# Two due times in a planned attention-plus-MLP kernel: VectorE's normalisations of the last pairs, and GpSimd's scales of the later batches

## The chip, the core and the metric

The kernel runs on one core of one Trainium2 chip. The metric is the device time of one execution in microseconds (us), as the median of several executions. One execution in each set was also profiled; all lines below come from those profiles. The names in the lines: PE is TensorE, PEld its weight loads, DVE is VectorE, ACT is ScalarE, POOL is GpSimd, SP is SyncE, which issues most transfers.

## The reference, cut to what matters

```python
q, k, v: (8, 12, 448, 64) float32          # batch, heads, tokens, head size
q_n, k_n = q / |q|, k / |k|
attn = softmax(q_n @ k_n.T / 0.1)           # per batch and head
x    = concat_heads(attn @ v)               # (3584, 768)
h    = x @ w_in                             # (768, 2048)
out  = (h * sigmoid(1.702 * h)) @ w_out     # (2048, 768)
```

## The kernel before

Two heads make a *pair*; a batch has six pairs, so pairs 0 to 5 are batch 0, 6 to 11 batch 1, and so on. For each pair: load k and q, square (ScalarE), sum (VectorE), take the root, invert, scale k and q to unit length, transpose, make the scores (TensorE), exponentiate (ScalarE), multiply with v (TensorE), normalise (VectorE), turn (TensorE), copy. When all pairs of a batch are there, the MLP takes its tokens. Batch 0 and 1 are worked in two halves of the tokens ("h" is 0 or 1), and the first MLP matmul of batch 0 is made in eight *units* for each half.

Nothing in the program decides the order by hand. A planner in the kernel simulates the engines before the program is written: each operation has an engine, an assumed duration, a due time, things it must follow, and slots that it takes and frees (PSUM banks, buffers, and a "port" shared by VectorE and GpSimd). Whenever an engine is free in that simulation, it gets the *ready* operation with the earliest due time. The result is a fixed order of instructions for each engine. In the cut below, `s` and `sh` are a pair's own place in time, `early` lies before it, `first` means a pair of batch 0, `URGENT` is 12; due times are in units of the plan, not in us, and a smaller one goes first.

```python
plan = Plan(dict(q=NQK, k=NQK, v=4, sq=3, qks=6, vt=NV, qkT=7, sp=2, a=1, exp=NE, xs=3, xf=3)
          | dict(x=2 * HP, mm=3, run=3, th=3, g0=KT2, g1=KT2, ost=2, port=1))   # mm: 3 PSUM banks, ost: 2 output buffers
...
add(("scale", ti, x), "DVE" if dve else "POOL", 0.7 if dve else 1.0,
    early + 0.5 if first else s - 5 - ti * 0.1, partial(scale, x, ti, ...),
    after=[("norm", 1, grp)], takes=[("qks", 1), ("port", 1)], frees=[(nm, 1), ("port", 1)])
...
if x == grp[0] and x in range(HP, PW):                # pairs 6 to 9: the root on GpSimd
    add(("norm", 0, grp), "POOL", 0.5 + 2.4 * n, early + 0.3, partial(power, grp), after=reds)
    add(("norm", 1, grp), "DVE", 0.45, early + 0.3, partial(inverse, grp), after=[("norm", 0, grp)], **port)
...
add(("nx", x, h), "DVE", 0.65, sh + 1 - (0 if first else URGENT), partial(normalise_h, x, h), after=[("at", x, h)], ...)
add(("turn", x, h), "PE", 0.15, sh + 1, partial(turn_h, x, h), after=[("nx", x, h)], ...)
add(("x", x, h), ..., 0.35, sh + 1 - (0 if first else URGENT), partial(turned_h, x, h), after=[("turn", x, h)], ...)
...
add(("ost", b2, t, n), "ACT", 0.4, due - URGENT, partial(halve, b2, t, n), after=after,   # evacuates an output tile
    takes=[("ost", int(n == 0))], frees=[("mm", 1)], ...)
add(("w_out", i), "POOL", 1.0, 3 + i, partial(load_w_out, i), ...)                         # two halves of w_out
```

In the lines, L581 is the first MLP matmul of batch 0, L534 and L552 that of the later batches, L611 the second MLP matmul, L484 the product with v, L507 the turn, L375 a dummy transpose ("fill") that the kernel issues to keep TensorE warm, L495 and L497 the normalisation, L517 the copy after the turn, L591 and L568 the gate (it frees a PSUM bank), L563 the tanh, L269 the sums of squares, L326 the root on GpSimd, L333 and L334 its inverse, L343 the scale, L623 the evacuation of an output tile.

## Time and profile before

| | before |
|---|---|
| time | 432.85 us, median of 3 (432.06 to 433.2) |
| TensorE busy | 98% of a span of 430.0 us, granted clock 1.00 |
| VectorE, ScalarE, GpSimd busy | 55%, 68%, 41% |
| fills on TensorE | 238, of these 47 after 44 us |
| TensorE from 100 us to the last matmul | full but for some tenths of a us |

The lines themselves, and what they leave to win, are in the prediction.

### The profile page before, as it was taken

To read this page: it belongs to the slowest core of one execution; us is meant where nothing else is said; L and a number is where in the kernel's file an instruction comes from. 1 tells how busy PE (TensorE), PEld (TensorE's weight loads), DVE (VectorE), ACT (ScalarE), POOL (GpSimd) and SP (SyncE) were. 2 spreads that over 40 slices of the span, in tenths; PEclk is the share of its full clock that TensorE was granted. 3 is DMA by queue.
4 is the path that set the end of the run, shared out by engine and by line. 5 is a ranking of instruction groups with operands and counts; after the bars stand their busy time and mean duration, and the time that the engine had idled before them with its cause. 6 is when DMAs were issued, how large, how long until landed. Compare 5 with 4: busy or idle time off the path is not lost.

```text
span 430.0 us, 11091 instructions
## 1 busy us (share of the span) xinstructions
PE 419.9 (98%) x4438; PEld 261.2 (61%) x4438; DVE 236.5 (55%) x621; ACT 290.5 (68%) x460; POOL 175.4 (41%) x229
## 2 busy tenths in 40 slices
PE   7889999999999999999999999999999999999996
PEld 7768886654565555555556556556656556555564
DVE  5875887877874577829656554553432433123200
ACT  5979679958877788887884886766673864233321
POOL 0830995297678847463682717260100000000000
PEclk9999999999999999999999999999999999999999
DMA  8999997968999999696979475845203021211122
GB/s 215 197 202 268 246 204 207 291 128 203 207 201 184 249 236 204 160 196 169 162 197 220 123 201 134 152 107 93 63 14 93 9 63 49 50 38 37 38 73 75
DMA packets 98099, 64.03 MB, mean 149 GB/s; under 512 B 56320, under 2 KB 93056, under 8 KB 98048
## 3 DMA queue, kind: packets, MB, share of 16 engines
q1 hardware_dynamic: 92320, 57.03, 58.2%
q0 software_dynamic: 5696, 6.29, 8.9%
q8 instruction: 35, 0.57, 0.5%
q14 instruction: 16, 0.13, 0.1%
q10 hardware_dynamic: 32, 0.01, 0.0%
HBM read 45.61 MB, written 11.01 MB: 132 GB/s over the span
## 4 chain that ended last, share of the span: by engine, by line
PE 86%; ACT 4%; DVE 3%; issue 2%; POOL 2%; DMA 1%; SPq 0%; ACTq 0%; POOLq 0%
PE mm L611 34%; PE mm L534 17%; PE mm L552 11%; PE avp L431 8%; PE sp L405 7%; PE sp L467 2%; PE mm L484 2%; ACT et L416 2%; PE mm L581 2%; DMA k<-in_k_dram 1%; ACT sq L263 1%; DVE n L269 1%; POOL qks L343 1%; PE tps L375 1%; POOL n L326 1%
## 5 line engine op out<-in xcount | busy, mean ns | idle before, releaser
L416 ACT ACTIVATE et<-sp 112x896 f16<-112x896 f32 x192 | 170.1, 919 | 29.7 <-PE sp L405 24.8
L611 PE MATMUL mm<-w_out,gT 128*128 128x384 f16 (+1 forms) x912 | 158.4, 323 | 0.0
L611 PEld LDWEIGHTS <-gT 128*128 128x128 f16 x912 | 83.9, 98 | 60.6 <-issue 11.0
L568 DVE SCALAR_TENSOR_TENSOR gT<-th,mm 128x448 f16<-128x448 f16 x112 | 67.0, 616 | 64.9 <-ACT th L563 64.8
L563 ACT ACTIVATE th<-mm 128x448 f16<-128x448 f32 x128 | 67.7, 550 | 39.3 <-PE mm L534 31.9
L534 PE MATMUL mm<-xT,w_in 128*128 128x448 f16 x408 | 85.2, 353 | 0.3 <-DVE gT L568 0.3
L269 DVE TENSOR_REDUCE n<-sq 112x8 f32<-112x512 f32 x96 | 63.9, 679 | 21.8 <-ACT sq L263 13.2
L623 ACT ACTIVATE ost<-mm 128x384 f32<-128x384 f32 (+1 forms) x57 | 27.8, 488 | 62.1 <-PE mm L611 61.7
L534 PEld LDWEIGHTS <-w_in 128*128 128x128 f16 x408 | 37.7, 98 | 36.8 <-issue 5.8
L552 PE MATMUL mm<-xT,w_in 64*128 64x448 f16 x528 | 57.1, 349 | 0.0
L359 POOL CAST vt<-v 112x256 f16<-112x256 f32 x90 | 34.0, 404 | 56.4 <-PE avp L431 42.2
L431 PEld LDWEIGHTS <-et 112*128 112x128 f16 x1152 | 43.6, 97 | 13.8 <-issue 3.7
L343 POOL TENSOR_TENSOR qks<-k,y 112x512 f16<-112x512 f32 x38 | 39.7, 1044 | 26.3 <-DVE y L310 12.9
L431 PE MATMUL avp<-vt,et 112*128 112x65 f16 x1152 | 47.0, 193 | 0.1
L442 DVE RECIPROCAL rcx<-avp 128x4 f32<-128x4 f32 x72 | 13.0, 180 | 61.7 <-PE avp L431 61.6
L262 POOL TENSOR_TENSOR sq<-q 112x512 f32<-112x512 f32 x33 | 34.2, 1041 | 29.4 <-DVE y L310 9.0
L405 PE MATMUL sp<-qkT 64*128 64x448 f16 x288 | 43.3, 353 | 0.0
L343 POOL TENSOR_TENSOR qks<-q,y 112x512 f16<-112x512 f32 x38 | 39.7, 1044 | 0.0
L552 PEld LDWEIGHTS <-w_in 64*128 64x128 f16 x528 | 25.6, 94 | 21.0
L263 ACT ACTIVATE sq<-k 112x512 f32<-112x512 f32 x48 | 30.3, 635 | 3.4 <-DMA k<-in_k_dram 3.4
L445 DVE TENSOR_TENSOR xf<-avp,rcx 128x256 f16<-128x256 f32 x72 | 30.6, 425 | 2.5
L405 PEld LDWEIGHTS <-qkT 64*128 64x128 f16 x288 | 13.4, 93 | 14.6 <-issue 6.7
(48 smaller groups left out, 277.6 us busy)
## 6 DMA issues: line engine op xcount, KB each, us to landing
k<-in_k_dram SPq DMA_DIRECT2D x48, 224.0 KB, 4.5
q<-in_q_dram SPq DMA_DIRECT2D x48, 224.0 KB, 5.0
v<-in_v_dram SPq DMA_DIRECT2D x48, 224.0 KB, 4.2
w_in<-in_moe_w_in_dram POOLq DMA_DIRECT2D x2, 1536.0 KB, 15.7
w_out<-in_moe_w_out_dram POOLq DMA_DIRECT2D x2, 1536.0 KB, 15.4
out_dram<-ost SPq DMA_DIRECT2D x7, 336.0 KB, 4.7
out_dram<-ost SPq DMA_DIRECT2D x8, 288.0 KB, 2.9
out_dram<-ost SPq DMA_DIRECT2D x8, 240.0 KB, 3.1
```

The costliest lines, as they stand in the source:

```text
L262: return nc.gpsimd.tensor_tensor(out=sqs[x, ti], in0=src, in1=src, op=ALU.mult)
L263: return nc.scalar.activation(out=sqs[x, ti], in_=src, func=AF.Square)
L269: nc.vector.tensor_reduce(out=n2s[grp][:, x - grp[0], ti], in_=sqs.pop((x, ti)), axis=AX.X, op=ALU.add,)
L343: return eng.tensor_tensor(out=qkss[x][:, 1 - ti].rearrange("p c j d -> p j c d"), in0=src, in1=rss[x][:, ti, :, :, None].to_broadcast((P, ...
L405: nc.tensor.matmul(out=sp[:, j, :S], lhsT=keys(x, j, c), rhs=queries(x, j, 0, S), start=True, stop=True,)
L416: nc.scalar.activation(out=e[:, : 2 * S].rearrange("p (j s) -> p j s", j=2), in_=sps.pop(key)[:P, :, :S], func=AF.Exp, scale=inv_tau, **kw,)
L431: nc.tensor.matmul(out=ps[:, (D + 1) * t : (D + 1) * (t + 1)], lhsT=exps[x, c][:, q0 : q0 + 128], rhs=values(x, c, D * j, D * j + D + 1), ...
L534: nc.tensor.matmul(out=ps[:, :S], lhsT=w_in_sb[:, kk, 128 * m : 128 * (m + 1)], rhs=xTs[b, kk][:, :S], start=(kk == 0), stop=(kk == KT1 - 1),)
L552: insts.append(nc.tensor.matmul(out=mms[b, m + i][:, :S], lhsT=w_in_sb[rows, kk, 128 * (m + i) : 128 * (m + i + 1)], rhs=xTs[b, kk][rows, :S],
L563: nc.scalar.activation(out=ths[key], in_=mms[key][:, :S], func=AF.Tanh, scale=0.851)
L568: nc.vector.scalar_tensor_tensor(out=gT[:, m, (b % 2) * S : (b % 2 + 1) * S], in0=ths.pop((b, m)), scalar=1.0, in1=mms.pop((b, m))[:, :S], ...
L611: nc.tensor.matmul(out=mms[b2, t, n][:, : c1 - c0], lhsT=gT[:, kk, 128 * t : 128 * (t + 1)], rhs=w_out_sb[:, kk, c0:c1], start=(kk == 0), ...
```

## The change

Two intents: let the last two pairs of batch 0 go first on VectorE, as the second half of the MLP of batch 0 waits for them; and on GpSimd let the scales of a pair go ahead of the root of the next.

```diff
-    PW = 10
+    PW = (6, 7, 8, 9)
...
-    groups += [(x,) for x in range(HP, PW)] + [tuple(range(PW, HALF))] * (PW < HALF)
+    groups += [(6,), (7,), (8,), (9,), (10, 11)]
...
-   ... early + 0.5 if first else s - 5 - ti * 0.1,          # due time of the scales
+   ... early + 0.5 if first else s - 8 - ti * 0.1,
...
-        if x == grp[0] and x in range(HP, PW):
+        if x == grp[0] and x in PW:
...
-   add(("nx", x, h), ..., sh + 1 - (0 if first else URGENT), ...
+   add(("nx", x, h), ..., sh + 1 - (0 if first and not (h and x >= HP - 2) else URGENT), ...
...
-   add(("x", x, h), ..., sh + 1 - (0 if first else URGENT), ...
+   add(("x", x, h), ..., sh + 1 - (0 if first and not (h and x >= HP - 2) else URGENT), ...
```

## The prediction

> **What bounds the kernel now.** I began with the page of the kernel before: busy shares and the slices.
>
> ```profile
> span 430.0 us, 11091 instructions
> PE 419.9 (98%) x4438; PEld 261.2 (61%) x4438; DVE 236.5 (55%) x621; ACT 290.5 (68%) x460; POOL 175.4 (41%) x229
> PE   7889999999999999999999999999999999999996
> PEclk9999999999999999999999999999999999999999
> ```
>
> TensorE is busy 419.9 of 430.0 us at full clock, so only 10.1 us of the span are open to any reordering. Splitting the span into stretches shows where they lie: 3.5 us in the first 20 us (before the change can act), 2.2 us between 20 and 50, 0.5 between 50 and 100, about 0.2 between 100 and 300, and 3.6 in the tail after the last matmul. From 100 us on there is nothing to win by order.
>
> Busy is not useful, though: the kernel issues dummy transposes of the identity (line 375) to keep TensorE warm while the plan sees it idle. They are 238 instructions, 18.1 us, of which 12.0 fall before 20 us, 2.9 between 20 and 40, and 3.3 between 44 and 52. So I read TensorE's timeline around 44 to 52 us, where the change acts (lines left out between):
>
> ```profile
> 44.68 0.22 PE L375 MATMUL tps<-ident 128*128 128x128 f16 x1
> 45.10 1.31 PE L581 MATMUL mm<-xT,w_in 128*128 128x224 f16 x12 [0.19 <-DVE gT L591]
> 46.24 0.65 PE L484 MATMUL mm<-vt,et 112*128 112x65 f16 x16
> 46.73 0.33 PE L375 MATMUL tps<-ident 128*128 128x128 f16 x3
> 47.27 1.31 PE L581 MATMUL mm<-xT,w_in 128*128 128x224 f16 x12 [0.20 <-DVE gT L591]
> 48.41 2.29 PE L375 MATMUL tps<-ident 128*128 128x128 f16 x38
> 50.66 0.27 PE L507 MATMUL mm<-ident,xs 112*128 112x112 f16 x2
> 50.77 0.44 PE L375 MATMUL tps<-ident 128*128 128x128 f16 x5
> 51.05 1.31 PE L581 MATMUL mm<-xT,w_in 128*128 128x224 f16 x12
> ```
>
> At 46.24 the last attention product of batch 0 (pair 5, second half) is made; at 47.27 the eighth and last unit of the first MLP matmul on the first half of the tokens. Then 38 fills stand in for 2.25 us of nothing, until the turn of pair 5 at 50.66. The units of the second half need all six pairs, so they begin at 51.05. What VectorE did meanwhile:
>
> ```profile
> 46.65 0.56 DVE L591 SCALAR_TENSOR_TENSOR gT<-th,mm 128x448 f16<-128x448 f16 x1
> 47.13 0.67 DVE L269 TENSOR_REDUCE n<-sq 112x8 f32<-112x512 f32 x1
> 47.72 0.61 DVE L591 SCALAR_TENSOR_TENSOR gT<-th,mm 128x448 f16<-128x448 f16 x1
> 48.25 1.27 DVE L269 TENSOR_REDUCE n<-sq 112x8 f32<-112x512 f32 x2
> 49.44 0.61 DVE L591 SCALAR_TENSOR_TENSOR gT<-th,mm 128x448 f16<-128x448 f16 x1
> 49.97 0.18 DVE L495 RECIPROCAL rch<-mm 112x4 f32<-112x4 f32 x1
> 50.18 0.42 DVE L497 TENSOR_TENSOR xs<-mm,rch 112x256 f16<-112x256 f32 x1
> ```
>
> The product is out at 46.9 (46.24 + 0.65); its normalisation starts at 49.97, 3.1 us late, behind three gates and three reductions of the next batch. Likewise pair 4: product at 41.16, normalised at 43.88, about 2 us late. GpSimd is the other queue concerned:
>
> ```profile
> 46.50 2.93 POOL L326 TENSOR_TENSOR n<-n,root_of 112x16 f32<-112x16 f32 x1
> 49.39 1.19 POOL L654 DMA_DIRECT2D w_out<-in_moe_w_out_dram  x1
> 50.60 1.06 POOL L343 TENSOR_TENSOR qks<-k,yv 112x512 f16<-112x512 f32 x1
> 51.61 1.05 POOL L343 TENSOR_TENSOR qks<-q,yv 112x512 f16<-112x512 f32 x1
> ```
>
> Pair 6, the first of batch 1, is scaled only after the root of pair 7 and a weight load, though its own inverse root was ready at about 46.65.
>
> **What the Trainium skill says.** "Perfetto Trace Analysis", Identifying the Most-Contended Engine, warns that matmul busy share is no measure of the distance to the limit; the trace agrees: 43 of the instructions that make the slice from 48.4 to 51.05 look full compute nothing. "TensorE: Matmul & The Clock Gate", Architectural detail, calls the queues of VectorE and ScalarE strictly first in, first out; so a priority in this kernel's planner is worth something only as an order of the program, and the normalisation above, ready at 46.9 and started at 49.97, waits just in that way. "SBUF — State Buffer", SBUF: two separate sides, describes a port pair shared by VectorE and GpSimd as an exclusive lock for a whole instruction. The trace fits: the inverse's add (line 333) took 0.17 us when GpSimd was free, but 0.71, 0.54 and 1.01 us beside GpSimd's work. The planner models this with its "port" token, which will matter below.
>
> **The change part by part.**
> The first two hunks change nothing: PW was 10, range(6, 10) is (6, 7, 8, 9), and the groups written out are those built before. Instructions and durations stay; only order moves.
>
> VectorE first for the second half of pairs 4 and 5. The pair's VectorE path is 0.18 + 0.42 us, the turn on TensorE, and a copy of 0.28. Started at about 46.9 (after the inverse that ends at 46.7), pair 5 has xs at 47.5, the turn at about 47.6, the copy at 48.1. The units of the second half can then follow at 48.4, when the last unit of the first half is issued, instead of 51.05: 2.65 us. For pair 4, 2 us earlier frees one of the three PSUM banks of the pool earlier; the small holes at 44.68 to 47.27 (4 fills at 0.06, and waits of 0.19 and 0.20 for a gate that frees a bank, 0.6 us in all) may shrink, but a normalisation ahead of a gate delays that gate by its 0.6 us. I count these two as cancelling, 0 to 0.3.
>
> Scales due 3 units earlier for all pairs from 6 on. A scale of 1.05 us twice per pair goes ahead of a root of 2.93 us and of the second weight load of 1.19 us where it is ready when GpSimd picks. In the planner pair 6 is not yet ready when the first weight load ends (the inverse is just running), so the root of pair 7 may well stay ahead; the load of 1.19 us is what is passed for sure, for pairs 7 and 8 perhaps the next root too. Visible TensorE waits that this can remove from 51 on: 0.15 us for the scale at 52.71, some 0.1 each at 60 and 68.3: 0.3 us. Its main use is to keep TensorE supplied once the MLP units are 2.65 us earlier. GpSimd is 97 to 100% busy from 44 to 62 us, so the first scores of batch 1 would otherwise not move. From pair 12 on the earlier scales only meet a TensorE that is full anyway: 0.
>
> Sum: 2.65 + 0.15 + 0.3 = 3.1 us, less 0.4 for new small waits = 2.7. TensorE is full from 53 us to the end, so the whole shift arrives at the end: 432.85 - 2.7 = 430.1 us.
>
> **The rivals.**
> (a) GpSimd becomes the bound: the units run out before batch 1's scores are ready. For: GpSimd is full in that stretch, and TensorE waited right behind its scales at 52.71 and 68.7. Against: eight units of 1.15 us (9.2 us) can run from 48.4, and pair 6's transposes come earlier. It would return 1 to 2.5 us: 431 to 432.7.
> (b) The second weight load goes behind the scales of pair 6, some 2.1 us later. It took 13.7 to 17.2 us to land, and the inputs of batch 2 are held for it: SyncE issues nothing from 48.14 to 66.64. The output matmuls, first at 65.61, need their weights. For: a shift forward of the matmuls and a delay of the load add up to almost 5 us. Against: the first group needs the first half of the weights only, and the scaled inputs of batch 2 are first worked on after 87 us. I give it 0.5 us of cost on average; at worst 2 us: 432.
> (c) ScalarE takes over: it is 92% busy from 40 to 50. But it idles 3.24 us from 49.1, waiting for the very units that now come early. Hence little; if it cost 1 us, 431.
> (d) More is won: a fully packed stretch from 44 to 53 removes 3.2 us of fills and waits there, plus other holes to 70 us, at most 4 us: 428.9. The clock cannot sink from fewer fills, as matmuls replace them; "TensorE: Matmul & The Clock Gate", What's actually happening, gives an idle window of some 3.4 us for a fall, and no such gap arises; the clock before was full throughout.
>
> **Range and chances.** 2% is 8.7 us. Faster than 424.2 would take more than every fill and hole after 20 us (2.9 + 3.3 + 2.2 + 0.5 = 8.9, most of them before the change acts), so 1.5%. Slower than 441.5 would need a plan that goes badly wrong; a changed static order allows that in principle, but TensorE has other work almost everywhere: 1.5%. The rest is within 2%. The range: rival (d) with some noise below, 428.4; rivals (a) and (b) with the runs' spread (432.06 to 433.2) above, 432.4.
>
> **What would show it.** Right: the normalisations of pair 5 start within 0.5 us of the product; the block of 38 fills is gone or under 10; the second half's first unit at about 48.4; TensorE's timeline from 70 us on is the same but 2 to 3 us earlier; fills fall from 238 to about 195; the span is near 427.3. Wrong: a new wait of TensorE on a scale, a gate or the output weights between 50 and 70 us, of the size of the fills removed; or the scales in the same places on GpSimd, which makes the second part idle. If TensorE shows new waits after 100 us, the early scales have broken the order of later batches.

## The result, and the profile after

The changed kernel took 429.76 us (median of 6, 429.62 to 431.45) beside 432.92 us of the kernel before (6 runs). A ratio here is the mean time of one kernel's runs over that of the other's of the same rounds, so it is not quite the ratio of the medians: 0.9943, with a 95% interval of 0.9921 to 0.9965. That is 2.5 us less of the means, 3.2 of the medians. In later rounds (e5 below) it was 0.9952, or 2.1 us.

The page of the changed kernel:

```profile
span 428.9 us, 11014 instructions
PE 418.8 (98%) x4404; PEld 259.7 (61%) x4404; DVE 235.4 (55%) x621; ACT 290.6 (68%) x460; POOL 175.2 (41%) x229
```

There are 34 matmuls fewer than before (4404 against 4438): 34 fills, at 0.06 us each 2.0 us. This profiled run was one of the slower ones (430.66 us), and its first 40 us run about 0.47 us later than in the profile before (the root of pair 6 starts at 42.80, not 42.33). So the times below are to be read with 0.47 taken off. TensorE's timeline where the fills had been (columns: start, duration, engine, line, what; in brackets the idle time before it and what ended it):

```profile
46.26 0.65 PE L484 MATMUL mm<-vt,et 112*128 112x65 f16 x16
46.74 0.78 PE L375 MATMUL tps<-ident 128*128 128x128 f16 x11
47.76 0.27 PE L507 MATMUL mm<-ident,xs 112*128 112x112 f16 x2 [0.24 <-DVE xs L497]
47.87 0.28 PE L375 MATMUL tps<-ident 128*128 128x128 f16 x2
48.28 3.61 PE L581 MATMUL mm<-xT,w_in 128*128 128x224 f16 x36
```

The block of 38 fills is gone, but a smaller hole has come where none of that size was: from 46.74, where the fills behind the product begin, to 48.28, only the turn is useful. And the three units that begin at 48.28 are not all of the second half: counted over the timeline, only seven units came before them, so the first of the three is still the eighth of the first half. The second half begins with the next unit, 1.15 us later, at about 49.43 (48.96 with the 0.47 taken off; before it was 51.05). VectorE shows why:

```profile
46.20 0.71 DVE L333 TENSOR_SCALAR yv<-n 112x16 f32<-112x16 f32 x1
46.95 0.25 DVE L334 RECIPROCAL yv<-yv 112x16 f32<-112x16 f32 x1
47.12 0.12 DVE L495 RECIPROCAL rch<-mm 112x4 f32<-112x4 f32 x1
47.27 0.42 DVE L497 TENSOR_TENSOR xs<-mm,rch 112x256 f16<-112x256 f32 x1
47.62 0.61 DVE L591 SCALAR_TENSOR_TENSOR gT<-th,mm 128x448 f16<-128x448 f16 x1
```

The normalisation of pair 5 now starts 0.2 us after its product (47.12 against 46.26 + 0.65), as planned. But the gate at 47.62, whose bank the eighth unit needs, now stands behind the inverse of pair 6 and that normalisation.

On GpSimd (same columns) the root of pair 7 is still ahead of pair 6's scales. What the scales have passed is the second half of w_out, which was at 49.39 before:

```profile
46.97 2.93 POOL L326 TENSOR_TENSOR n<-n,root_of 112x16 f32<-112x16 f32 x1
49.87 1.04 POOL L343 TENSOR_TENSOR qks<-k,yv 112x512 f16<-112x512 f32 x1
50.87 1.03 POOL L343 TENSOR_TENSOR qks<-q,yv 112x512 f16<-112x512 f32 x1
51.86 1.24 POOL L654 DMA_DIRECT2D w_out<-in_moe_w_out_dram  x1
```

Both scales of pair 7 (from 56.02) also come before the root of pair 9 (58.03); before, that root lay between them. From 52 to 70 us TensorE is busy 18.00 of 18 us, against 17.68 before.

A count of TensorE's losses in the two profiles: from 44 to 52 us, fills and waits fell from 47 x 0.06 + 0.19 + 0.20 = 3.2 us to 13 x 0.06 + 0.24 + 0.13 = 1.15; from 52 to 70 a further 0.32 us went. A new wait of 0.36 us came at 94, for the evacuation of an output tile, where before there was one of 0.15 at 97, and two new ones of 0.15 us came at 191 and 218. The sum, some 1.9 us, is a little under the timed 2.1 to 2.5.

So far the result looks much as predicted. The experiments show that the gain is kept for a reason that the prediction did not have.

### The profile page after: what moved, and what is told of

Its sections match the earlier page's. It is cut to its first block, busy times and chain, and to the rows that moved or that the text cites. A ratio compares the mean times of both kernels' runs of the same rounds, so it can differ in the third digit from the quotient of the medians.

```text
span 428.9 us, 11014 instructions
## 1 busy us (share of the span) xinstructions
PE 418.8 (98%) x4404; PEld 259.7 (61%) x4404; DVE 235.4 (55%) x621; ACT 290.6 (68%) x460; POOL 175.2 (41%) x229
## 4 chain that ended last, share of the span: by engine, by line
PE 86%; ACT 4%; DVE 4%; issue 2%; POOL 2%; DMA 1%; SPq 0%; POOLq 0%; ACTq 0%
PE mm L611 33%; PE mm L534 18%; PE mm L552 11%; PE avp L431 8%; PE sp L405 7%; PE mm L581 3%; PE sp L467 2%; PE mm L484 2%; ACT et L416 2%; POOL qks L343 1%; DMA k<-in_k_dram 1%; DVE n L269 1%; PE tps L367 1%; PE tps L375 1%; ACT sq L263 1%
## 5 line engine op out<-in xcount | busy, mean ns | idle before, releaser
L611 PE MATMUL mm<-w_out,gT 128*128 128x384 f16 (+1 forms) x912 | 159.0, 323 | 0.2 <-DVE gT L568 0.2
L611 PEld LDWEIGHTS <-gT 128*128 128x128 f16 x912 | 83.6, 98 | 60.7 <-issue 11.8
```

The lines of the kernel that those rows point to most:

```text
L611: nc.tensor.matmul(out=mms[b2, t, n][:, : c1 - c0], lhsT=gT[:, kk, 128 * t : 128 * (t + 1)], rhs=w_out_sb[:, kk, c0:c1], start=(kk == 0), ...
```

## The experiments

Ten kernels ran, each for five rounds beside the kernel before on the same chip, each with a correct result. "Before" in the table is its median in the same rounds.

| run | edit | time, us | before, us | ratio | 95% interval |
|---|---|---|---|---|---|
| e1_control | first two hunks alone | 432.42 | 432.06 | 0.9996 | 0.9971 to 1.0021 |
| e2_vector_first_only | VectorE part alone | 433.85 | 432.06 | 1.0028 | 1.0005 to 1.0051 |
| e3_scales_only | scales part alone | 433.86 | 432.06 | 1.0046 | 1.0015 to 1.0078 |
| e4_scales_batch1 | both, scales for pairs 6 to 11 only | 429.11 | 432.06 | 0.9925 | 0.9902 to 0.9947 |
| e5_change_again | the change | 429.96 | 432.56 | 0.9952 | 0.9927 to 0.9978 |
| e6_vector_first_3_out | e2 with 3 output buffers | 431.23 | 432.56 | 0.9979 | 0.9962 to 0.9997 |
| e7_before_3_out | before with 3 output buffers | 434.56 | 432.56 | 1.0046 | 1.0018 to 1.0073 |
| e8_best | e4, 3 buffers, a later inverse | 428.94 | 432.56 | 0.9926 | 0.9907 to 0.9945 |
| e9_pair5_first | e4, pair 5 alone first | 432.00 | 431.86 | 1.0002 | 0.9981 to 1.0023 |
| e10_pair4_first | e4, pair 4 alone first | 431.41 | 431.86 | 0.9988 | 0.9970 to 1.0007 |

There is noise that the table does not show. About a third of the executions have a mean granted clock of 0.994 to 0.996 (one 0.990) instead of 0.998 to 1.00, and in the kernel before these were 0.7 to 1.5 us longer in the mean. Four of the profiles are such (e1, e2, e7, e8). In each of them TensorE's clock was 0.83 from 10 to 20 us, against 1.00 in the profile before, and the first L581 came at 34.6 to 35.1 us instead of 32.6 to 33.6; so the loss lies ahead of the place of the change. With the executions at 0.998 and above alone, the means lie beside that of the kernel before at -2.9 us (e4), -2.6 (e5), -3.4 (e8), -1.2 (e6), +1.5 (e2), +1.7 (e3), and within 0.5 us for e1, e9 and e10, so the readings below stand. Only e7 has too few of them: one of six, at 432.54 us beside 432.28.

### e1: the hunks that change nothing

The edit is the two hunks on PW and the groups. The programs were compared instruction by instruction: the order is the same on all engines.

> The kernel before with only the first two hunks (the way the groups are written). Every instruction on every engine is in the same order as before, so all theories expect the same time, within 0.2% (0.9 us). What it shows otherwise is the noise that the other differences have to be held against.

The ratio was 0.9996. So differences of a quarter of a per cent have to be read with their intervals.

### e2: only VectorE first

```diff
  the change, and
-   early + 0.5 if first else s - 8 - ti * 0.1
+   early + 0.5 if first else s - 5 - ti * 0.1
```

> Only pairs 4 and 5 of batch 0 first on VectorE; the scales keep their old due times. Theory (as predicted): this part carries the gain. The block of 38 fills shrinks to some 11, a gain of about 2 us, and only 0.3 us of the gain of the change is missing: 430 to 431 us. Rival: an earlier MLP part alone is given back between 85 and 100 us, where TensorE then has nothing but the first matmuls of batch 1 and waits for a PSUM bank (1 to 1.5 us of new waits there): then 432 to 433, no faster than before, and the early scales would be what makes the gain keep.

The rival was right: 433.85 us, 0.28% *slower* than before. The fills are gone just as in the change (13 left after 44 us). But here are TensorE's waits of this kernel from 36 us to the end, in total (columns: who waited for whom, us, times, longest):

```profile
PE mm L534 <- DVE gT L568: 2.0, 3, 1.3
PE mm L507 <- DVE xs L497: 0.8, 2, 0.5
PE mm L611 <- DVE gT L568: 0.6, 1, 0.6
```

The first and last rows are waits for gates that free a bank: 1.29 us at 97, and 0.61 us each at 204 and 217 us. The first in TensorE's timeline:

```profile
93.95 2.11 PE L611 MATMUL mm<-w_out,gT 128*128 128x384 f16 x12
95.90 1.30 PE L534 MATMUL mm<-xT,w_in 128*128 128x448 f16 x6
98.48 4.70 PE L534 MATMUL mm<-xT,w_in 128*128 128x448 f16 x24 [1.29 <-DVE gT L568]
```

and ScalarE at the same time:

```profile
97.23 0.54 ACT L563 ACTIVATE th<-mm 128x448 f16<-128x448 f32 x1 [2.02 <-PE mm L534]
97.67 0.87 ACT L623 ACTIVATE ost<-mm 128x384 f32<-128x384 f32 x2
```

The pool has three PSUM banks. Two hold the two halves of the third output tile (L611); they are freed by the evacuations at 97.67. Those stand behind a tanh, for whose matmul ScalarE idled 2.02 us. So the first units of batch 1's MLP ran through one bank: matmul, tanh, gate, and only then the next matmul. In the changed kernel the order is the other way round:

```profile
93.64 0.87 ACT L623 ACTIVATE ost<-mm 128x384 f32<-128x384 f32 x2
95.51 0.54 ACT L563 ACTIVATE th<-mm 128x448 f16<-128x448 f32 x1 [1.00 <-PE mm L534]
```

Both evacuations come before the next tanh, and TensorE waits only 0.36 us. The third tile may be evacuated only when the first tile's buffer is free, as there are two. In e2 the first tile's store was issued in two parts at 84.60 and 85.48, and both had landed at 90.96; in the change they were issued at 80.41 and 80.80 and had landed at 86.83. So in e2 the buffer was free 6.7 us before the evacuations. The order is the planner's: its simulation, run by itself, issues the second part in e2 at 81.3 us of its own time and starts the third tile's evacuation at 94.9, behind the tanh at 93.7. For the change it has 79.3 and 92.1, ahead of the tanh at 93.9. So it reckons with some 13 us from issue to a free buffer, where the chip took 5.5 to 6.2, and a tanh that comes earlier than that is put first.

### e3: only the scales early

```diff
  the change, and
-   sh + 1 - (0 if first and not (h and x >= HP - 2) else URGENT)      # both nx and x
+   sh + 1 - (0 if first else URGENT)
```

> Only the scales due 3 units earlier for all pairs from 6 on; VectorE as before. Theory: the 38 fills and the normalisation 3.1 us late stay, so at most 0.3 us faster: 432.3 to 433. Rival: the scales carry the gain: 430 to 431. A third way: the new order alone costs, because TensorE changes more often between its 64-row and 128-row matmuls (about 0.11 us for a pair of changes in the trace): 433.5 to 435.

433.86 us, 0.46% slower: the third way in its direction, but not in its cause. Changes between 64-row and 128-row matmuls were 178 in TensorE's timeline against 176 before, worth 0.1 us. What is new is waits; three rows of the same view as above:

```profile
PE avp L431 <- DVE xf L445: 0.8, 1, 0.8
PE mm L611 <- DVE gT L568: 0.4, 1, 0.4
PE tps L367 <- POOL qks L343: 0.4, 1, 0.4
```

The last begins at 51.4 us, where pair 6's transposes come too early for its scale; the others lie between 210 and 230 us. 42 of the 47 fills stay. In the books below the waits are 1.6 us more than before and the whole is 1.5 us more.

### e4: early scales only for batch 1

```diff
  the change, and
-   s - 8 - ti * 0.1
+   s - (8 if x < HALF else 5) - ti * 0.1
```

> The whole change, but the scales are early only for pairs 6 to 11 (batch 1); from pair 12 on they are due as before. Theory: from pair 12 on TensorE is full anyway, so the time is that of the change, 429.8 within 0.5 us. Rival: part of the gain comes from the later batches: then 430.5 to 432.

429.11 us: all of the gain, and perhaps a little more (the intervals of e4 and of the change overlap). From pair 12 on the early scales bring nothing.

Three more programs were only compared, not run. With the scales of batch 1 two units early instead of three, the program is instruction for instruction that of e2. With three units for pairs 7 to 11 it is again e2. With three units for pair 6 alone it is e4. So of the whole second part one thing acts: pair 6's scales, due at 3.9 and 4.0 instead of 6.9 and 7.0, pass the second half of w_out, due at 4. All else on GpSimd follows from it.

### e5, e6, e7: is it the output buffer?

```diff
  e6: e2, e7: the kernel before, each with
-   p_o = pool("p_o", 2)      ost=2
+   p_o = pool("p_o", 3)      ost=3
```

> The changed kernel once more, on the chip and in the rounds of the three below, as their measure: 429 to 430.5 us, some 2.5 us under the kernel before.

> VectorE first for pairs 4 and 5 alone (as in e2, scales late), but with three output buffers in place of two. Theory after e2: alone, the first part loses its 2 us of removed fills to a wait of 1.29 us at 97 us, where two of the three PSUM banks hold the third output tile, whose evacuation is ordered behind the landing of the first tile's store. With a third buffer that wait is gone and the gain shows: 430 to 431.5 us, at least 1.5 us under e2. Rival: what is short at 97 us is work, as the first scores of batch 2 come no earlier than 100 us; then the wait moves and the time stays at 432.5 to 434.

> The kernel before with three output buffers and nothing else. Theory: it waits only 0.15 us at 97 us, so the buffer brings nothing by itself: 432 to 434 us. Rival: output buffers bound the kernel in general, and it gains over 1 us.

The change again took 429.96 us. With a third output buffer the VectorE part alone (e6) took 431.23 us, 0.21% faster than before, and by the ratios (0.9979 / 1.0028) 0.5% or 2.1 us under e2. The wait at 97 us is gone, and so are those at 204 and 217. ScalarE evacuates the first half of the third tile as soon as it is there:

```profile
90.78 0.49 ACT L623 ACTIVATE ost<-mm 128x384 f32<-128x384 f32 x1 [2.12 <-PE mm L611]
```

So the rival of this step, that work is short at 97 us, falls. But 1.3 us of the change's gain (431.23 against 429.96) are still missing in e6, and neither waits nor fills account for them: e6 has the largest rest in the books below. The same buffer added to the kernel before (e7) made it 0.46% slower by the ratio: the waits of 0.61 and 0.60 us at 204 and 217 us appear there too. Part of the ratio can be the clock, as five of its six executions are of the lower one; its profile is 1.2 us longer from the first L581 to the last L611, which the start does not touch. The gain of over 1 us that a general bound by output buffers would give did not come, and the expected "nothing" is doubtful too. A resource that relieves one order can disturb another.

### e8: can the change be bettered?

```diff
  e4 with 3 output buffers (as in e6), and
-   partial(inverse, grp), after=[("norm", 0, grp)]
+   partial(inverse, grp), after=[("norm", 0, grp)] + [("nx", HP - 1, 1)] * (x == HP)
```

> The change with scales early for batch 1 only, three output buffers, and the inverse root of pair 6 put after the normalisation of pair 5 on VectorE. In the changed kernel TensorE lost 1.5 us between 46.7 and 48.3: the last unit of the first half waited for a bank whose gate stood behind a reduction, that inverse (0.71 us, held up by the descriptors of a weight load on GpSimd) and the normalisation. Theory: that hole shrinks to about 1 us or less, and the 0.36 us at 94 goes, so 0.5 to 1.5 us under the changed kernel. Rival: the hole shrinks and the gain is lost again at a later wait: the same as the changed kernel within 0.5 us.

428.94 us, 0.74% under the kernel before and 1.0 us in the median under the change of the same rounds; the intervals of the two still overlap. Against e4, in other rounds, no gain is shown at all (0.9926 beside 0.9925), so the third buffer and the later inverse are not shown to do more than make the hole smaller. TensorE:

```profile
47.73 0.65 PE L484 MATMUL mm<-vt,et 112*128 112x65 f16 x16
48.22 0.22 PE L375 MATMUL tps<-ident 128*128 128x128 f16 x1
48.66 1.31 PE L581 MATMUL mm<-xT,w_in 128*128 128x224 f16 x12 [0.23 <-DVE gT L591]
49.81 0.26 PE L507 MATMUL mm<-ident,xs 112*128 112x112 f16 x2
49.91 0.61 PE L375 MATMUL tps<-ident 128*128 128x128 f16 x8
```

The eighth unit now follows 0.44 us after the product's slot ends (48.66 against 48.22), and 9 fills are left instead of 13. The wait at 94 us is gone. (This profile started late: its times are to be read with some 1.9 us taken off beside the profile before.) A wait of 0.46 us for a scale of pair 6 came at 54.6 in exchange.

### e9, e10: which pair

```diff
  e4, and in both due times
-   not (h and x >= HP - 2)
+   not (h and x == HP - 1)        # e9: pair 5;   e10: x == HP - 2, pair 4
```

> As e4 (scales early for batch 1), but only pair 5 goes first on VectorE; pair 4 as in the kernel before. Prediction's step: the 38 fills are pair 5's, so pair 5 alone carries the gain and pair 4 adds 0 to 0.3 us: 429 to 430. Rival, after the traces so far: with pair 4 late, the last units of the first half come later, so the fills go but a wait at 93 to 97 us returns as in e2 (1.3 us) and more behind it: 430.5 to 433.

> As e4, but only pair 4 goes first on VectorE; pair 5 as in the kernel before. Both views expect the block of some 38 fills before the turn of pair 5 to stay. Prediction: hardly any gain, 432 to 433.5. Rival: pair 4 and the early scales carry most of the gain, then 430 to 431.

Pair 5 alone (e9): 432.00 us, no gain. The block of 38 fills falls to 10, and the old wait is back, with 0.60 us more at 215:

```profile
95.83 4.70 PE L534 MATMUL mm<-xT,w_in 128*128 128x448 f16 x24 [1.29 <-DVE gT L568]
```

Pair 4 alone (e10): the 38 fills stay, as both views expected, and the time is 431.41 us, within noise of before. Neither pair carries the gain alone.

### The books of all runs

From the start of the first MLP matmul (L581) to the end of the last one (L611), a profile's time can be split into TensorE's waits, the fills (0.06 us each), and the rest:

| profile | us from first L581 to last L611 | waits | fills | rest |
|---|---|---|---|---|
| before, e1 | 393.2, 393.2 | 1.4, 1.2 | 47, 47 | 389.0, 389.1 |
| change, e5 | 391.7, 391.2 | 1.5, 1.6 | 13, 13 | 389.5, 388.9 |
| e2, e3 | 394.1, 394.7 | 3.5, 3.0 | 13, 42 | 389.8, 389.1 |
| e4, e8 | 390.7, 390.3 | 1.3, 1.4 | 13, 9 | 388.6, 388.3 |
| e6, e7 | 392.3, 394.4 | 1.5, 2.5 | 13, 47 | 390.0, 389.1 |
| e9, e10 | 393.4, 393.0 | 3.2, 1.4 | 14, 47 | 389.4, 388.8 |

The rest is the same within 0.85 us either way, so waits and fills explain most of the larger differences. What moves the rest is not settled. Changes of row mode (144 to 154 in this stretch, at about 0.11 us for a pair) can account for some 0.5 us of it. And the change and e5, one program, differ by 0.6: 0.4 of this are three matmuls at 154 to 159 us that started 0.11 to 0.17 us later after the one before them than in e5, with no idle time shown. So the rest holds small waits too. The start of the first L581 itself lies between 32.6 and 35.1 us from profile to profile, before any part of the change acts, so single spans must not be compared to within 1 us.

## Why the prediction was right or wrong

The time, 430.1 against 429.76 us, lay well within the range of 428.4 to 432.4, and the class (within 2%) was right. Step by step:

- *Only the first 100 us are open, and 2% is out of reach*: right. The ten experiments lie between 0.75% faster and 0.46% slower than before.
- *The first hunks change nothing*: right (e1).
- *VectorE first wins 2.65 us, for pair 5*: the mechanism was right (normalisation 0.2 us after the product instead of 3.1), the size was not. The prediction took the first half's last unit as fixed at 47.27. In fact its gate was pushed back by the normalisation, and the second half began at about 48.96 (with the 0.47 taken off), not 48.4. The prediction named this delay but called it cancelled. Measured for 44 to 52 us: 2.0 to 2.1 us. Its own signs say the same: 11 fills of the block are left (it said under 10) and 204 in all (it said about 195).
- *Pair 4 adds 0 to 0.3 us*: wrong. Without it (e9) the gain was zero; the two pairs cannot be added up.
- *The scales: 0.3 us from 51 on, mainly to keep TensorE supplied with scores*: the visible waits were sized right (0.32 us from 52 to 70), and the second weight load was passed, as it said for sure. But the use was misjudged. Without them (e2) the change loses 0.76 to 0.86% by the ratios (1.0028 over 0.9952 or 0.9943), some 3.5 us. Between the profiles it is 2.4 to 2.9 us, of which 2.0 are waits: 0.9 us for the order of an output tile's evacuation at 94 to 98 us, and 1.1 us at 204 and 217, whose cause was not traced. Supply of scores is not among them.
- *TensorE is full from 53 us to the end, so the whole shift arrives at the end*: this is the step that failed, as a statement on its own. A full engine in one order does not stay full in another. In e2, e3 and e9, 1.6 to 2.5 us of waits between 90 and 230 us (1.29 us at 97 and 1.22 at 204 and 217 in e2) ate what was won. In the change it held because both parts together happened to give an order with only small waits later. For this the prediction had no reason; it was luck.
- *From pair 12 on: 0*: right (e4).
- *Rival (a), GpSimd as the bound*: not in the change; no wait on a scale is left from 36 us on. *Rival (b), w_out later*: its issue moved by 2.5 us (49.39 to 51.86; 2.0 with the 0.47 taken off), but SyncE's loads, which wait for it, moved only from 66.64 to 66.91, no later once the 0.47 is taken off, so the cost was near zero. The share of the transfer engines was 1.1 to 1.3 from 44 to 62 us in both profiles; that they were full is a likely reason, but it was not tested. *Rival (c), ScalarE*: right to dismiss; its 3.24 us of idle time shrank to pauses of 0.6 to 1.1.
- *The add takes 0.17 us when GpSimd is free*: half read. The add at 18.69 us took 0.17 us too, and GpSimd was then writing the descriptors of a transfer (18.55 to 19.38); see the last section.

So the number came out right because in the changed kernel the sum holds nearly as predicted: 1.9 us counted and 2.1 to 2.5 timed, for 2.7. The error does not show in it: each part by itself costs 1 to 2 us. The prediction has this only as a sign of being wrong (new waits after 100 us), not as a term of its sum. A theory tested on the changed kernel only would have passed.

## What to carry to other kernels

Where a planner fixes all orders at once, the parts of a change are not additive: both halves of this one slow the kernel by 0.3 to 0.5% and together speed it up by 0.5%. Before crediting a hole that was closed, look along the bounding engine to the end of the program for the hole that opens, and ask which buffers and banks that engine's next work needs. Check the durations that the planner assumes against the chip: here a store reckoned at twice its time put a tanh ahead of an evacuation. And compare the orders of the instructions: they show without a run that a due time three units earlier mattered in one place, against a transfer that the change's intent did not mention.

## What the Trainium skill lacked or had wrong

- "SBUF — State Buffer", SBUF: two separate sides, has the shared port pair locked for the whole GpSimd instruction. Beside a scale (1.05 us) the add of the inverse was indeed held, until 0.03 to 0.04 us after the scale's end (0.54 and 1.01 us in the kernel before), but beside the root of 2.93 us it took its free 0.17 us (changed kernel: the add at 53.44 within the root of 53.12 to 56.04). So not every GpSimd instruction held it off to its end.
- The same page warns that VectorE can hold up the descriptors of a transfer issued by GpSimd, and does not speak of the reverse for descriptors. These runs fit the reverse, in part: in the changed kernel the add at 46.20, 0.5 us into descriptor work (45.70 to 46.94), took 0.71 us and ended at 46.91. The add at 19.17, 0.14 us into other descriptor work (19.03 to 19.86), took its free 0.17 us.
- "TensorEngine Tiling (Array Packing)", Key Properties, says that a change of tiling mode drains TensorE, and gives no figure for it. In the chain of waits of the kernel before, four matmuls of the second MLP layer took 0.76 us right after 64-row scores and 0.65 us elsewhere: 0.11 us. From start to start it is the same: a group of four 64-row score matmuls took 0.48 us between 128-row matmuls and 0.38 us among 64-row ones.
- No page speaks of how an order fixed in advance behaves when one part of it is moved; here new waits of 0.6 to 1.3 us opened 50 to 170 us after the place of the edit.
